# Block-sparse attention with a mixer MLP on one Trainium2 core: values of the later pairs by SyncE's queue and a GpSimd cast, and early value loads behind casts

## The chip, the cores and the metric

The kernel runs on 1 core of one Trainium2 chip. The metric is the time of one execution on the device, in microseconds (us). Engines are named as in the profile: PE (TensorE matmul), PEld (its weight loads), DVE (VectorE), ACT (ScalarE), POOL (GpSimd) and SP (SyncE, which only issues transfers here). Each engine works through its own list of instructions in order. Transfers are issued by SP and by POOL; both feed the same 16 DMA engines.

## The reference, cut to what matters

The first part is attention for 4 batches of 8 heads, 768 rows of 64; each query attends to the three best of its key blocks of 64 rows and to its own block, causally. The second is a token and channel mixer over its result.

```python
k_rep = k.reshape(B, H, n_blocks, block, D).mean(axis=3)
gate_scores = np.einsum('bhsd,bhnd->bhsn', q, k_rep)       # top 3 causal blocks + own block -> mask
scores = scale * np.matmul(q, k.transpose(0, 1, 3, 2))     # masked, causal
attn = np.exp(scores - max); attn = attn / sum
x = np.matmul(attn, v)                                     # -> (4, 768, 512)
h = np.maximum(x.transpose(0, 2, 1) @ w_tok1, 0.0) @ w_tok2
u = x + h.transpose(0, 2, 1)
out = u + np.maximum(u @ w_ch1, 0.0) @ w_ch2
```

q, k, v and the weights come as float32; the kernel computes in float16 with float32 sums.

## The kernel before

The work is cut into 16 pairs of heads, `pairs[i] = (b, h)`, numbered 0 to 15; four pairs make a batch. For each pair `prepare(i)` makes these operations:

- **Loads.** SP loads the keys `kl` and the queries `ql` as float32 (L313, two transfers of 192 KB each, one for each head; runs of 256 bytes). POOL loads the values `V` (L320, one transfer that casts to float16 on the way, straight into `V16[i % 6]`).
- **Transposes.** PE transposes `kl` and `ql` (L358, six blocks each) into a PSUM tile of the ring `big`, which has two places. ACT copies it to `kt` or `qt` (L367; rings of two and four). POOL casts `kt` and `qt` to float16 into `KA` and `QA` (L374, two casts each, one for each head).
- **Gate.** DVE sums blocks of keys (L387, L395), PE multiplies (L405, or L415 and L435 for groups of pairs), DVE finds the third best block (L447 to L483), PE turns the mask (L493) and DVE puts it into `QA` (L499).

`attend(i)` follows: scores on PE (L513), exponentials on ACT (L526), the diagonal mask on DVE (L533), `e` times `V` on PE (L545), and the division (L553, L564). The mixer of a finished batch (`tok1` L576 and L607, `umix` L588 and L621, `ch1` L657, `ch2` L678) is interleaved on PE with the attention of later pairs; its weights come by ten POOL transfers that also cast (L706, L707, L709, L711), one of 768x256, one of 256x768, four of `wc1` and four of `wc2`.

No loop sets the order. `plan()` works it out when the program is built: it takes the operations with their dependences, an occupation in ns, a due time (`prio`) and the rings that they take, and starts on each engine what is ready first, ties within 60 ns going to the smaller due time. A transfer has a `size`, which is the time that the planner gives it on the DMA engines; `transfers()` shares them between POOL's and SP's queue by `SHARE`. `casts` after `WAIT[n]` hold each weight transfer back; a line after the loops holds each value load behind a transpose of queries, `O["tr", "ql", d]`. SP's operations are started strictly in the order of due times. Where PE has nothing ready, the planner puts in multiplications of a tile of zeros (L695, tile `warm`); they stand in PE's list from then on. The resulting order is emitted under a manual schedule, so on the chip each engine follows it whatever the actual times are; the waits come from the tiles' uses. Each transfer by SP waits for the one eight places before it on SP's queue, since eight semaphores go round.

Two rings matter around the change: `V16` has six places, so the values of pair i can't be written before `e` times `V` of pair i-6 is done; `kt` has two, so the copy to `kt` of pair i waits for both casts of pair i-2.

Of the kernel before, what the change touches and what calls it, by code (L numbers as in the profile page):

```python
# [9 lines left out]
FP = mybir.dt.float32  # L10
# [18 lines left out]
R = 5  # L29
NBN = 4  # L30
# [9 lines left out]
def QACT(i):  # L40
    return i < 1


GATE = {2: 700, 3: 700, 4: 730}
GROUPED = [[0], [1], [2], [3], [4], [5], [6, 7], [8, 9, 10, 11], [12, 13, 14, 15]]
WAIT = [("kt", 3, 1), ("kt", 3, 1), ("qt", 3, 1), ("qt", 3, 1), ("qt", 4, 1), ("qt", 4, 1),
        ("qt", 5, 1), ("qt", 5, 1), ("qt", 6, 1), ("qt", 6, 1)]
# [171 lines left out]
def kernel(  # L219
# [11 lines left out]
    nc = tc.nc  # L231
    B, H, S, D = q.shape
    NB = S // 64
    NJ = S // 128
# [12 lines left out]

    pairs = [(b, h) for b in range(B) for h in range(0, H, 2)]
    NP = len(pairs)
    RINGS = dict(big=2, bank=3, av=1, ql=3, kl=3, qt=4, kt=2, gs=1, gt=1, gm=1, m8=1, bn=NBN, e0=3, e1=3, e2=3, rc=2,  # L250
                 x16=2, h1=2, u=2, uT=2, h2=1, ob=3)

    def sb(tag, shape, dt, name):
        return sp.tile(shape, dt, tag=tag, bufs=RINGS[tag], name=name)

    def ps(tag, shape, name, dt=FP):
        if tag == "big":
            return pp.tile([128, 1024], FP, tag=tag, bufs=RINGS[tag], name=name)
        return pp.tile(shape, dt, tag=tag, bufs=RINGS[tag], name=name)


    avp = pp.tile([128, 512], FP, tag="av", bufs=1, name="avp")
    V16 = [sp.tile([128, 2, NJ, 65], F16, tag=f"V{r}", name=f"V{r}") for r in range(R + 1)]
# [23 lines left out]
    T = {}  # L287
# [3 lines left out]
    def op(eng, occ, rec, deps, prio, fn, takes=(), size=0):  # L291
        o = Op(eng, occ, rec, deps, prio, fn, takes, size)
        ops.append(o)
        return o

    def pe(occ, deps, prio, fn, takes=(), tail=170):
        return op("PE", occ, occ + tail, deps, prio, fn, takes)

    def act(cols, deps, prio, fn, takes=()):
        return op("ACT", 70 + cols * 0.833, 173 + cols * 0.833, deps, prio, fn, takes)  # L300
# [5 lines left out]
    def load_qk(i, t32, src):  # L306
        b, h = pairs[i]

        def f():
            t = sb(t32, [128, NJ, 2 * D], FP, f"{t32}_{i}")  # L310
            T[t32, i] = t
            for g in range(2):
                nc.sync.dma_start(out=t[:, :, D * g:D * g + D], in_=src[b, h + g].rearrange("(j p) d -> p j d", p=128))  # L313
        return f

    def load_v(i):
        b, h = pairs[i]

        def f():
            nc.gpsimd.dma_start(out=V16[i % (R + 1)].rearrange("p g j d -> p (g j) d")[:, :, 0:D],  # L320
                                in_=v[b, h:h + 2].rearrange("g (j p) d -> p (g j) d", p=128))
        return f


    def load_gate_consts():
# [195 lines left out]
    def expo(i, x, g):  # L521
        def f():
            width = GROUPS[g][0]
            e = sp.tile([128, 1024 if g < 2 else 640], F16, tag=f"e{g}", bufs=RINGS[f"e{g}"], name=f"e{g}_{i}_{x}")
            T["e", i, x, g] = e
# [23 lines left out]
    def recip(i, x):  # L549
        def f():  # L550
            rc = sp.tile([128, NJ, 1], FP, tag="rc", bufs=RINGS["rc"], name="rc")
            T["rc", i, x] = rc
            nc.vector.reciprocal(out=rc.rearrange("p n o -> p (n o)"),  # L553
                                 in_=T["aps", i, x][:, :, 64:65].rearrange("p n o -> p (n o)"))
# [143 lines left out]
    O = {}  # L698
# [13 lines left out]
    W = []  # L712

    def prepare(i):
        b, h = pairs[i]
        gi = [n for n, G in enumerate(GROUPED) if i in G][0]
        i0 = GROUPED[gi][0]
        pre = 10.0 * (i0 - (AHEAD if i < FIRST else LATER)) + 2.5 * (i - i0) - (0 if len(GROUPED[gi]) == 1 else EXTRA)
        vpre = 10.0 * (i - (AHEAD if i < FIRST else LATER))
        old = i - R  # L720

        def last_scores(x):
            return [O.get(("sc", old, x, g)) for g in range(3)]

        for t32, src, off in (("kl", k, 0), ("ql", q, 0.1)):
            bf = Buf(t32)
            O[t32, i] = op("SP", 950, 0, [], pre - 12 + off, load_qk(i, t32, src), [bf], size=1750)
            big = Buf("big")
            O["tr", t32, i] = pe(660, [O[t32, i]], pre + off, transposes(t32, i), [big], tail=320)
            bf.users.append(O["tr", t32, i])  # L730
            name = "kt" if t32 == "kl" else "qt"
            tb = Buf(name)
            O[name, i] = act(768, [O["tr", t32, i]],
                             pre + 0.5 + off, evac_t(t32, i), [tb])
            big.users.append(O[name, i])
            dst = KA if name == "kt" else QA
            for x in range(2):
                occ = 770
                if QACT(i):
                    O["cast", name, i, x] = act(768, [O[name, i]] + last_scores(x), pre + 0.9 + 0.2 * x + off, cast_act(dst, name, i, x))  # L740
                    tb.users.append(O["cast", name, i, x])
                    continue
                O["cast", name, i, x] = op("POOL", occ, occ + 55, [O[name, i]] + last_scores(x), pre + 4 + off,
                                           cast(dst, name, i, x))
                tb.users.append(O["cast", name, i, x])
            if name == "kt":
                O["ksum", i] = dve(870, [O["kt", i]], pre + 1, ksum(i))
                tb.users.append(O["ksum", i])
                O["kcopy", i] = dve(200, [O["ksum", i], O.get(("gate", old))], pre + 1, kcopy(i))
            else:  # L750
                qb = tb
        O["v", i] = op("POOL", 1060, 0, [O.get(("av", i - R - 1, x)) for x in range(2)], vpre + 2, load_v(i), size=1350)
        n = len(GROUPED[gi])
        O["qb", i] = qb
        if i == GROUPED[gi][-1]:
            G = GROUPED[gi]
            if n == 1:
                gb = Buf("bank")
                O["gate", i] = gate_op = pe(1120, [O["kcopy", i], O["qt", i]], pre + 2, gate(i), [gb])
            else:  # L760
                tbig = Buf("big")
                gate_op = pe(GATE[n], [O["kcopy", m] for m in G] + [O["qt", m] for m in G], pre + 2, gate_t(gi), [tbig])
                for m in G:
                    O["gate", m] = gate_op
                gtb = Buf("gt")
                ge = act(S - 128, [gate_op], pre + 2.1, gate_e(gi), [gtb])
                tbig.users.append(ge)
                gb = Buf("big")
                gback = pe(550, [ge], pre + 2.2, gate_b(gi), [gb])
                gtb.users.append(gback)  # L770
            for m in G:
                O["qb", m].users.append(gate_op)
            gs = Buf("gs")
            O["gm", gi] = dve(75 + 125 * n, [gate_op] if n == 1 else [gback, own_op], pre + 3, gm(gi), [gs])
            gb.users.append(O["gm", gi])
            tops = [dve(720, [O["gm", gi]], pre + 3, top(gi, s)) if s == 0 else None for s in range(n)]
            for s in range(1, n):
                tops[s] = dve(720, [tops[0]], pre + 3, top(gi, s))
            O["lt", gi] = dve(75 + 125 * n, tops, pre + 3, below(gi))
            O["bias", gi] = dve((75 + 125 * n) if n == 4 else 200 * n, [O["lt", gi], O.get(("mask", gi - NBN))] + ([own_op] if n == 4 else []), pre + 3, bias(gi))  # L780
            gs.users += [O["bias", gi]]
            O["lt", gi].two = O["bias", gi].two = True
            mb = Buf("bank")
            O["mask", gi] = pe(280, [O["bias", gi]], pre + 4, mask(gi), [mb])
            for s, m in enumerate(G):
                for x in range(2):
                    O["put", m, x] = dve(410, [O["mask", gi]] + [O.get(("sc", m - R, x, g)) for g in range(3)],
                                         pre + 4, put_mask(gi, s, x))
                    mb.users.append(O["put", m, x])
# [38 lines left out]
        for i in G:  # L828
            attend(i)

    for i, d in enumerate((1, 2, 2, 3, 3, 4, 4, 5, 6, 7, 8, 9, 10, 11, 12, 13)):
        O["v", i].deps.append(O["tr", "ql", d])
    own_op.deps.append(O["cast", "qt", 4, 1])
    for x in range(2):
        O["cast", "kt", 0, x].deps.append(O["qt", 0])
    O["ksum", 1].deps.append(O["bias", 0])
    for n, (at, f) in enumerate(wq):
        W.append(op("POOL", 700, 0, [O[("cast",) + WAIT[n]]], at, f, size=4500 if n < 2 else 2100))

    for b in range(B):  # L840
        fill = 1000.0 * (b + 1)
# [5 lines left out]
        if b == 0:  # L847
            for c in range(4):
                bk = Buf("bank")
                at = fill + c  # L850
# [65 lines left out]
    kernel_plan.update(ops=O)  # L916
    order, span = plan(ops, RINGS)

# [65 lines left out]
```

The softmax here doesn't subtract the row's maximum and nothing guards it: scores larger than these inputs give would overflow.

## Time and profile before

| what | us |
|---|---|
| median of 12 runs | 265.87 |
| lowest and highest of them | 265.2 and 268.87 |
| the profiled execution's own time | 267.72 |
| its span in the trace | 265.6 |
| PE busy | 255.7 (96%) |
| DVE, ACT, POOL busy | 159.1, 145.2, 80.0 |
| SP's queue: packets, MB, share of 16 DMA engines | 63232, 21.33, 39.1% |
| POOL's queue: the same | 28064, 7.08, 27.0% |

The span is the trace's; the rest of an execution's own time lies before its first and after its last instruction. Lines of the profile name an instruction by its line of the kernel, engine, and tiles written and read. A DMA share is the sum of the packets' times over the 16 engines, divided by the time, so it exceeds 1 where packets of two queues overlap. MB and GB/s count the bytes as written, so a transfer of values to float16 counts half of what it reads.

### The profile page before, as it was taken

To read this page: it belongs to the slowest core of one execution; us is meant where nothing else is said; L and a number is where in the kernel's file an instruction comes from. 1 tells how busy PE (TensorE), PEld (TensorE's weight loads), DVE (VectorE), ACT (ScalarE), POOL (GpSimd) and SP (SyncE) were. 2 spreads that over 40 slices of the span, in tenths; PEclk is the share of its full clock that TensorE was granted. 3 is DMA by queue.
4 is the path that set the end of the run, shared out by engine and by line. 5 is a ranking of instruction groups with operands and counts; after the bars stand their busy time and mean duration, and the time that the engine had idled before them with its cause. 6 is when DMAs were issued, how large, how long until landed. Compare 5 with 4: busy or idle time off the path is not lost.

```text
span 265.6 us, 5842 instructions
## 1 busy us (share of the span) xinstructions
PE 255.7 (96%) x2304; PEld 166.2 (63%) x2304; DVE 159.1 (60%) x536; ACT 145.2 (55%) x195; POOL 80.0 (30%) x112
## 2 busy tenths in 40 slices
PE   7889999999996999999999999999999999999994
PEld 7777888895765767455666676655456544456443
DVE  4668869896974769986547975493233153333222
ACT  3757898677894966457873599860024400044000
POOL 8494819849445745225520000000000000000000
PEclk9999999999999999999999999999999999999999
DMA  8999999999997999059511000009220026310032
GB/s 170 204 169 189 177 180 208 192 188 193 192 151 141 211 205 174 21 78 171 69 45 41 1 2 0 2 0 187 92 79 2 0 46 152 119 41 0 2 141 96
DMA packets 91322, 28.77 MB, mean 108 GB/s; under 512 B 84896, under 2 KB 87840, under 8 KB 91296
## 3 DMA queue, kind: packets, MB, share of 16 engines
q1 hardware_dynamic: 63232, 21.33, 39.1%
q0 software_dynamic: 28064, 7.08, 27.0%
q8 instruction: 18, 0.29, 0.5%
q14 instruction: 8, 0.07, 0.1%
HBM read 26.83 MB, written 6.29 MB: 125 GB/s over the span
## 4 chain that ended last, share of the span: by engine, by line
PE 86%; DMA 8%; SPq 3%; DVE 2%; issue 1%; DVEq 0%
PE c L678 23%; PE c L657 23%; PE sps L513 13%; DMA kl<-in_k_dram 8%; PE avp L545 7%; PE ups L588 3%; PE tkl L358 3%; PE tql L358 3%; PE tok L576 2%; SPq L313 2%; PE gps L405 2%; PE gtp L415 1%; PE tok L607 1%; PE bps L493 1%; PE avp L695 1%; PE ups L621 1%
## 5 line engine op out<-in xcount | busy, mean ns | idle before, releaser
L526 ACT ACTIVATE e<-sps 128x1024 f16<-128x1024 f32 (+1 forms) x96 | 84.3, 920 | 17.3 <-PE sps L513 14.0
L657 PE MATMUL c<-uT,wc 128*128 128x256 f16 (+1 forms) x384 | 69.1, 326 | 0.0
L678 PE MATMUL c<-wc,h 128*128 128x512 f16 (+2 forms) x300 | 65.6, 370 | 0.0
L667 ACT ACTIVATE h<-c 128x512 f16<-128x512 f32 x48 | 28.7, 598 | 61.1 <-PE c L657 42.9
L657 PEld LDWEIGHTS <-wc 128*128 128x128 f16 x384 | 36.5, 97 | 23.0 <-issue 0.2
L513 PE MATMUL sps<-QA,KA 88*128 88x512 f16 (+3 forms) x256 | 50.1, 305 | 0.0
L678 PEld LDWEIGHTS <-h 128*128 128x128 f16 x300 | 28.7, 98 | 30.5 <-issue 1.0
L533 DVE TENSOR_TENSOR e<-e,m 128x256 f16<-128x256 f16 x90 | 30.0, 341 | 14.3 <-ACT e L526 13.8
L374 POOL CAST KA<-kt 64x768 f16<-64x768 f32 x30 | 24.7, 824 | 45.8 <-ACT kt L367 28.8
L686 DVE TENSOR_TENSOR ob<-u,c 128x512 f32<-128x512 f16 (+2 forms) x25 | 16.5, 664 | 32.1 <-PE c L678 32.1
L669 DVE TENSOR_SCALAR h<-c 128x256 f16<-128x256 f32 x48 | 20.3, 422 | 25.7 <-PE c L657 25.3
L513 PEld LDWEIGHTS <-KA 88*128 88x128 f16 x256 | 23.1, 99 | 17.0 <-issue 0.7
L374 POOL CAST QA<-qt 64x768 f16<-64x768 f32 x30 | 25.6, 852 | 6.1 <-ACT qt L367 4.7
L545 PEld LDWEIGHTS <-e 128*128 128x128 f16 x672 | 25.4, 97 | 2.8
L545 PE MATMUL avp<-V,e 128*128 128x65 f16 x672 | 26.7, 193 | 0.0
L367 ACT COPY kt<-tkl 128x768 f32<-128x768 f32 x16 | 12.8, 799 | 14.8 <-PE tkl L358 7.2
L387 DVE TENSOR_REDUCE kst<-kt 128x12 f32<-128x768 f32 x16 | 15.2, 950 | 8.2 <-ACT kt L367 8.0
L564 DVE TENSOR_TENSOR x<-avp,rc 128x384 f16<-128x384 f32 x32 | 17.8, 555 | 0.8
L320 POOL DMA_DIRECT2D V<-in_v_dram x16 | 16.5, 1035 | 5.6 <-PE avp L545 3.4
L358 PE MATMUL tkl<-id,kl 128*128 128x128 f32 x96 | 13.6, 277 | 4.2 <-DMA kl<-in_k_dram 4.2
L499 DVE COPY QA<-bps 24x640 f16<-24x640 f16 x32 | 14.3, 480 | 2.2 <-PE bps L493 1.9
L367 ACT COPY qt<-tql 128x768 f32<-128x768 f32 x16 | 12.8, 802 | 3.7 <-PE tql L358 3.5
(66 smaller groups left out, 212.3 us busy)
## 6 DMA issues: line engine op xcount, KB each, us to landing
kl<-in_k_dram SPq DMA_DIRECT2D x32, 192.0 KB, 5.7
ql<-in_q_dram SPq DMA_DIRECT2D x32, 192.0 KB, 5.8
out_dram<-ob SPq DMA_DIRECT2D x23, 256.0 KB, 2.0
V<-in_v_dram POOLq DMA_DIRECT2D x16, 192.0 KB, 8.5
wc<-in_moe_w_ch_dram POOLq DMA_DIRECT2D x8, 384.0 KB, 12.4
w<-in_moe_w_tok_dram POOLq DMA_DIRECT2D x2, 384.0 KB, 9.8
out_dram<-ob SPq DMA_DIRECT2D x1, 160.0 KB, 1.8
out_dram<-ob SPq DMA_DIRECT2D x1, 96.0 KB, 1.7
```

Of the source, the lines that this page charges most:

```text
L358: nc.tensor.transpose(out=p[:, 128 * j:128 * j + 128], in_=t[:, j, :], identity=ident32)
L367: nc.scalar.copy(out=t, in_=p[:, 0:S])
L374: nc.gpsimd.tensor_copy(out=to, in_=src)
L513: nc.tensor.matmul(out=p[:, off + a:off + a + n], lhsT=KA[i % R][x][0:MK, 128 * kk:128 * kk + 128], rhs=QA[i % R][x][0:MK, q0 + a:q0 + a + ...
L526: nc.scalar.activation(out=e[:, 0:width], in_=T["sps", i, x, g][:, 0:width], func=AF.Exp, scale=scale)
L533: nc.vector.tensor_tensor(out=d, in0=d, in1=m0.rearrange("p (a b) -> p a b", a=1).broadcast_to([128, 2, 128]), op=ALU.mult)
L545: nc.tensor.matmul(out=p[:, jq, :], lhsT=T["e", i, x, g][:, o:o + 128], rhs=V16[i % (R + 1)][:, x, kk, :], start=(kk == 0), stop=(kk == jq))
L564: nc.vector.tensor_tensor(out=T["x16", b][:, :, 64 * hh:64 * hh + 64], in0=T["aps", i, x][:, :, 0:64], in1=T["rc", i, x].broadcast_to([128 ...
L657: nc.tensor.matmul(out=p, lhsT=wc1_16[:, cc, 128 * fc:128 * fc + 128], rhs=T["uT", b][:, cc, a // 128:e // 128, :], start=(cc == 0), stop= ...
L667: nc.scalar.activation(out=T["h2", b][:, fc, a:e], in_=T["c1", b, fc, n], func=AF.Relu)
L669: nc.vector.tensor_scalar(out=T["h2", b][:, fc, a:e], in0=T["c1", b, fc, n], scalar1=0.0, scalar2=None, op0=ALU.max)
L678: nc.tensor.matmul(out=T["c2", b, j, lo], lhsT=T["h2", b][:, fc, 128 * j:128 * j + 128], rhs=wc2_16[:, fc, lo:hi], start=(fc == 0), stop=( ...
```

## The change

Three things change. The values of pairs 8 to 15 are loaded as float32 by SP into a new ring `v32` with two places (in SP's order right after the queries of the same pair), and POOL casts them into `V16`. The values of pairs 0 to 7 still come by POOL with the cast on the way, but each now waits for a given cast on POOL (`VAFTER`) instead of a transpose of queries. The `size` with which the planner counts the later weight transfers goes from 2100 to 2400 (`wc1`) and 2800 (`wc2`).

```diff
+VHW = 8
+VAFTER = [("kt", 1), ("kt", 2), ("qt", 2), ("qt", 3), ("qt", 3), ("kt", 4), ("qt", 4), ("qt", 5)]
...
-    RINGS = dict(big=2, bank=3, av=1, ql=3, kl=3, qt=4, kt=2, gs=1, gt=1, gm=1, m8=1, bn=NBN, e0=3, e1=3, e2=3, rc=2,
+    RINGS = dict(big=2, bank=3, av=1, ql=3, kl=3, qt=4, kt=2, v32=2, gs=1, gt=1, gm=1, m8=1, bn=NBN, e0=3, e1=3, e2=3, rc=2,
...
         def f():
-            nc.gpsimd.dma_start(out=V16[i % (R + 1)].rearrange("p g j d -> p (g j) d")[:, :, 0:D],
-                                in_=v[b, h:h + 2].rearrange("g (j p) d -> p (g j) d", p=128))
-        return f
+            src = v[b, h:h + 2].rearrange("g (j p) d -> p (g j) d", p=128)
+            if i < VHW:
+                nc.gpsimd.dma_start(out=V16[i % (R + 1)].rearrange("p g j d -> p (g j) d")[:, :, 0:D], in_=src)
+                return
+            T["v32", i] = sb("v32", [128, 2 * NJ, D], FP, f"v32_{i}")
+            nc.sync.dma_start(out=T["v32", i], in_=src)
+        return f
+
+    def cast_v(i):
+        return lambda: nc.gpsimd.tensor_copy(out=V16[i % (R + 1)].rearrange("p g j d -> p (g j) d")[:, :, 0:D], in_=T["v32", i])
...
-        O["v", i] = op("POOL", 1060, 0, [O.get(("av", i - R - 1, x)) for x in range(2)], vpre + 2, load_v(i), size=1350)
+        last_av = [O.get(("av", i - R - 1, x)) for x in range(2)]
+        if i < VHW:
+            O["v", i] = op("POOL", 1060, 0, last_av, vpre + 2, load_v(i), size=1350)
+        else:
+            vb = Buf("v32")
+            O["vl", i] = op("SP", 700, 0, [], pre - 11.8, load_v(i), [vb], size=1750)
+            O["v", i] = op("POOL", 820, 870, [O["vl", i]] + last_av, vpre + 2, cast_v(i))
+            vb.users.append(O["v", i])
...
-    for i, d in enumerate((1, 2, 2, 3, 3, 4, 4, 5, 6, 7, 8, 9, 10, 11, 12, 13)):
-        O["v", i].deps.append(O["tr", "ql", d])
+    for i, (name, m) in enumerate(VAFTER[:VHW]):
+        O["v", i].deps.append(O["cast", name, m, 1])
...
-        W.append(op("POOL", 700, 0, [O[("cast",) + WAIT[n]]], at, f, size=4500 if n < 2 else 2100))
+        W.append(op("POOL", 700, 0, [O[("cast",) + WAIT[n]]], at, f, size=4500 if n < 2 else 2400 if n < 6 else 2800))
```

## Prediction

> **What bounds the kernel now.** I read the busy times first, then the chain of waits, then PE's idle time, then the DMA engines in stretches of 4 us. PE is 96% busy, so what can be won is its idle time and its filler.
>
> ```profile
> PE 255.7 (96%) x2304; PEld 166.2 (63%) x2304; DVE 159.1 (60%) x536; ACT 145.2 (55%) x195; POOL 80.0 (30%) x112
> ...
> PE tkl L358 <- DMA kl<-in_k_dram: 4.2, 3, 2.3
> ```
>
> PE waits for a load of keys three times, 4.2 us together. The chain shows the places: before the transposes of pairs 2, 10 and 15.
>
> ```profile
> 7.54 6.09 DMA kl<-in_k_dram
> 13.77 0.85 PE tkl L358 x6
> ...
> 75.09 8.69 DMA kl<-in_k_dram
> 83.92 0.84 PE tkl L358 x6
> ...
> 99.52 6.13 DMA kl<-in_k_dram
> 105.79 0.84 PE tkl L358 x6
> ...
> 135.15 0.66 PE tql L358 x6
> ```
>
> The waits are 1.37, 2.34 and 0.46 us. The last line is the transposes of pair 15's queries, 29 us after its keys: PE asks for those late. From 107 to 144 PE shows 36.97 busy of 37 us, and from 144 to 181 36.97 of 37. So what PE loses up to 107 it doesn't get back, and what it gains it keeps.
>
> The DMA engines, by stretches (the last column is GB/s):
>
> ```profile
> 4.00:8.00 4.00, 3.81 (x52) 3.50 (x51) 1.27 (x3) 1.52 (x3) 4.00 (x5) 1.00 1.30 231
> 72.00:76.00 4.00, 4.00 (x43) 2.60 (x42) 3.70 (x10) 3.06 (x5) 3.82 (x5) 1.00 1.19 139
> 76.00:80.00 4.00, 4.00 (x47) 2.86 (x46) 2.39 (x8) 3.93 (x6) 0.25 (x1) 1.00 1.43 170
> 80.00:84.00 4.00, 1.66 (x31) 1.56 (x30) 2.24 (x7) 1.50 (x2) 2.60 (x4) 1.00 0.69 126
> 84.00:88.00 4.00, 4.00 (x29) 2.74 (x30) 2.31 (x5) 3.16 (x5) 2.46 (x4) 1.00 0.94 194
> 88.00:92.00 4.00, 4.00 (x37) 3.01 (x36) 2.72 (x6) 3.76 (x6) 2.60 (x4) 1.00 0.93 190
> 92.00:96.00 4.00, 4.00 (x50) 2.16 (x47) 2.33 (x6) 3.15 (x5) 3.19 (x4) 1.00 1.23 227
> 96.00:100.00 4.00, 4.00 (x49) 3.39 (x47) 2.92 (x25) 2.31 (x5) 1.01 (x1) 1.00 1.60 192
> 100.00:104.00 4.00, 4.00 (x32) 3.28 (x31) 4.00 (x26) 2.16 (x3) 3.61 (x4) 1.00 1.55 198
> ```
>
> SP alone moves 227 to 231 GB/s when it doesn't stop (4 to 8, 92 to 96). Beside values by POOL, whose float16 bytes count half, a full stretch shows 192 to 198. The DMA engines are thus full nearly all of the time up to 105, and short of it only from 72 to 92. Both bounds meet at 100 to 107: PE and the loads finish the attention's inputs together.
>
> **What a value load costs on each queue.** By SP, 393 KB (two times 192 KB) at 229 GB/s are 1.72 us of all engines. By POOL: from 96 to 104 the engines wrote 1560 KB; the loads of pairs 12 and 13 (issued 94.3 and 98.7, landed 5.9 and 6.6 later) lie nearly whole in it with 393 KB; the other 1167 KB at 229 are 5.1 us, which leaves 2.9 us for two, 1.45 each. Moving one from POOL to SP thus *adds* 0.27 us of DMA work. The Trainium skill weighs in here, "DMA: Bandwidth & Descriptors", section "Issuing engines are not separate DMA queues": transfers of all issuing engines interleave on the same 16 engines, so moving one saves issue time only. By that rule the price would be 0 a load instead of 0.27, and the sum below 1.6 us lower.
>
> **First part, early values held back.** Before, values 0 go out at 7.01 and share the engines with keys 2. After, in the order of the built program, POOL issues them after three casts: 11.87 + 3 x 0.85 = 14.4. Keys 2 (second half issued at about 7.4) come without them: values 0 had 5.5 us from issue to the last byte, and 1.45 us of that was theirs, so keys 2 land up to 1.4 sooner; PE's filler ends at 12.33, so 1.2 of the 1.37 is won. Values 0 then land at 14.4 + 6.0 (the row of values 1, issued at 15.29) = 20.4. PE wants them at 21.75 before; after, 1.2 sooner, but behind 7 + 1 instead of 2 multiplications of zeros (6 x 0.054) and keys 3's transposes (0.69), at 21.5. The cover is 1 us; between the fastest and slowest lone row (4.2 and 6.4) they land at 18.6 to 20.8. Values 1 and 2 are wanted after 29 and land at 25 to 28. PE's list has 128 multiplications of zeros for 136: 8 x 0.054 = 0.43 us less. First part: PE is 1.6 us ahead at 60 (0.5 to 2.4: values 0 late by 1; or also the 0.8 us of waits for DVE at 20.13 and 50.77 gone). All of it is only a lead; whether it lasts is decided below.
>
> **Second part, POOL's casts.** No value cast is in the trace. Nearest are the casts of 64x768 float32, 0.82 and 0.85 us. I take 0.85, since a partition has as many elements; bounds 0.82, and 1.7 if twice the partitions took twice as long. Each takes the place of an issue of 1.02 us: 8 x (0.85 - 1.02) = -1.4 us of POOL, bounds -1.6 and +5.4, and POOL is 30% busy. Not the length counts but the wait ahead: a cast of values stands in POOL's list until its load has landed. The list runs values 8, 9, keys and queries 8, values 10, 11, keys and queries 9 and 10, values 12, and so on. Keys 9 free a place of `kt`, and ACT's copy of keys 11 waits for it, with the exponentials queued behind. SP's list is queries 11, then values 11. Before, queries 11 land at about 89.3 (issued until 85.8, 4.1 to landing). After, values 8 to 11 add 4 x 0.27 = 1.1, and DMA idle time got back (below) takes 1.8: values 11 land at 88.6, their cast and the two of keys 9 end at 91.2, ACT copies keys 11 at 91.2 instead of 90.01. Before, PE goes on with scores at 91.28; after, it needs that copy done, 92.0, with 0.66 us of `e` times `V` done ahead. So here the lead of 1.6, and the 2.34 won at keys 10 (which go ahead of values 10 and 11), is spent: at 92 PE is level, +0.1 us (bounds -2 to +1.7, with the landing 2 sooner or the casts 1.7 long).
>
> **Third part, the end of the loads.** In PE's list the transposes of queries 15 now come right after those of keys 15, not 29 us later. In the old program that place is 105.79 + 0.68 = 106.4, and the end of those transposes would be 107.1. Before, queries 15 landed at about 106.6 (issued 100.23 to 101.5, 6.2 and 5.2 to landing), and nothing waited. What is different in DMA work ahead of them:
> - values 14, which before are issued at 120, are now ahead in SP's list: +1.72 us;
> - values 8 to 13 by SP: 6 x 0.27 = +1.6;
> - idle time of 72 to 92 that may be got back: 4 x (1 - 126/227) = 1.8 at 80 to 84, 1.2 and 0.6 at 72 to 80 against 198, 0.6 and 0.6 at 84 to 92: 4.8 us in all.
>
> How much of the 4.8 returns is the unknown. From 72 to 84 (3.6 us) values by POOL flew beside SP, which the change removes, but SP's own issues also stood up to 5 us there; from 84 to 92 SP was alone and still 15% short, so that share stays. I take half of the first: 1.8; bounds 0 and 4.8. Queries 15 land at 106.6 + 1.7 + 1.6 - 1.8 = 108.1 (105.1 to 109.9), their transposes end 0.1 + 0.66 later at 108.9, against 107.1: **+1.8 us** (level or ahead at the lower bound, +3.6 at the upper). PE's order behind it is dense as before, so this stays to the end. The weights' new sizes only shift places in the list: the ten transfers and their bytes are the same, and `wc2`, wanted at 101, landed at 74 before; 27 us cover it. Cost 0.
>
> **Sum.** In the profile's terms 265.6 + 1.8 = 267.4 of span. That execution took 267.72 (2.1 around the span), 1.85 above the median of 265.87; the difference goes on the median: 265.87 + 1.8 = **267.7**.
>
> **Rivals.**
> - *Idle time returns in full, faster.* With POOL's values gone SP runs at 227 throughout. Then values 11 land 2 us sooner, queries 15 at 105.1, and PE keeps a lead: filler 0.43, keys 2 1.2, keys 10 2.34, keys 15 0.46, together 4.4, less 1 to 2 at keys 11. 265.9 - 3 = 262.9. For: 92 to 96 at 227. Against: 84 to 92. Chance 0.28.
> - *Gains and waits cancel.* Three fifths to four fifths of the 4.8 return: queries 15 land within 0.7 us of where PE wants them, 265.2 to 267. So does a change that only exchanges one queue for the other, by the rule above. Chance 0.22.
> - *POOL's list is the stop, slower.* If casts of values take 1.7 us or values 9 and 11 land 2 us later than reckoned, keys 8 and 9 are cast later, ACT stands at the copies of keys 10 and 11 and PE with it: 2 x 0.85 + 2 = 3.7 more in that stretch, of which the lead has already been spent: 269.6. It decides once values 11 land after 90. Chance 0.12.
> - The forecast, queries 15 late by 0.5 to 3: chance 0.38.
>
> About 0.5% (1.3 us) is what a measurement of this kernel tells from no change. Faster by more 0.28, within 0.22, slower 0.50 (the forecast and POOL's stop). Range 262.8, just below the rival's 262.9, to 270.6 (3.6 of late queries and 1.1 of POOL).
>
> **What would show it.** The trace after should show keys 2's wait under 0.4 us; no wait of PE for keys 10; ACT's copy of keys 11 after a cast on POOL; a wait of PE before transposes of queries at 105 to 109; GB/s from 72 to 104 near 200. I am wrong if PE doesn't wait there (SP's queue was faster than I price it), or if `e` times `V` of pair 0 waits for values 0, or if GB/s stays at 225 from 70 on.

## The result and the profile after

| | before | after |
|---|---|---|
| median | 266.48 (47 runs, 265.15 to 268.87) | 270.01 (11 runs, 268.07 to 271.82) |
| ratio | | 1.0127, interval 1.0098 to 1.0156 |
| the profiled execution: own time, span | 267.72, 265.6 | 270.01, 268.0 |

The change makes the kernel 1.3% slower: +3.5 us, where +1.8 was forecast.

First the busy times, the queues and PE's waits of the changed kernel (line, what it waited for, us in all, times, longest):

```profile
PE 255.5 (95%) x2296; PEld 165.9 (62%) x2296; DVE 160.3 (60%) x536; ACT 145.1 (54%) x195; POOL 78.8 (29%) x112
...
q1 hardware_dynamic: 75648, 24.48, 45.9%
q0 software_dynamic: 15648, 5.51, 17.5%
...
PE tql L367 <- DMA ql<-in_q_dram: 3.5, 3, 1.7
PE sps L522 <- ACT kt L376: 2.2, 1, 2.2
...
PE tkl L367 <- DMA kl<-in_k_dram: 0.6, 1, 0.6
```

PE's own work is the same as before, 255.5 us against 255.7. What changed is what it stands still for: keys cost 4.2 us before and 0.6 now, but queries cost 3.5 and scores that stand behind ACT's copy of keys another 2.2, both new. The timeline of PE says where (start, duration, and in brackets the idle time ahead and what ended it; transposes of keys are `tkl`, of queries `tql`):

```profile
67.87 0.82 PE L367 MATMUL tkl<-id,kl 128*128 128x128 f32 x6
70.43 0.85 PE L367 MATMUL tql<-id,ql 128*128 128x128 f32 x6 [1.75 <-DMA ql<-in_q_dram]
...
81.29 0.82 PE L367 MATMUL tkl<-id,kl 128*128 128x128 f32 x6
...
92.02 0.59 PE L522 MATMUL sps<-QA,KA 88*128 88x512 f16 x3 [2.23 <-ACT kt L376]
98.29 0.85 PE L367 MATMUL tkl<-id,kl 128*128 128x128 f32 x6
...
103.92 0.85 PE L367 MATMUL tql<-id,ql 128*128 128x128 f32 x6 [0.74 <-DMA ql<-in_q_dram]
106.96 0.85 PE L367 MATMUL tkl<-id,kl 128*128 128x128 f32 x6 [0.62 <-DMA kl<-in_k_dram]
108.78 0.85 PE L367 MATMUL tql<-id,ql 128*128 128x128 f32 x6 [0.97 <-DMA ql<-in_q_dram]
```

These are pair 8 (the first two lines), keys 10, the scores at the copy of keys 11, keys 12, queries 14, and keys and queries 15. Keys 8 start at 67.87, 2.0 us ahead of the 69.90 of before; the lead is gone at queries 8, one line down. At keys 12 PE is where it was before, 98.29 against 98.23. The two lines of before:

```profile
69.90 0.87 PE L358 MATMUL tkl<-id,kl 128*128 128x128 f32 x6
...
98.23 0.85 PE L358 MATMUL tkl<-id,kl 128*128 128x128 f32 x6
```

The last three stops, 2.33 us together, put the end of pair 15's transposes at 108.78 + 0.69 = 109.5, and nothing behind it makes that good: 109.5 - 107.1 = 2.4 is the whole difference of the two spans.

The chain of waits shows what stands behind the two large stops (start, duration, what):

```profile
57.22 13.08 DMA ql<-in_q_dram
...
82.57 5.96 DMA v<-in_v_dram
...
88.66 0.83 POOL V L331
89.49 0.77 POOL KA L383
...
90.31 0.84 POOL KA L383
...
91.17 0.81 ACT kt L376
...
92.02 0.59 PE sps L522 x3
...
104.47 4.18 DMA ql<-in_q_dram
...
108.78 0.85 PE tql L367 x6
```

From 82.57 to 92.02 one can read the new dependence as a single line of work: values 11 land, POOL casts them, only then casts the two heads of keys 9, ACT copies keys 11 into the place that this frees, PE goes on. PE won't need values 11 until much later; they only stand ahead of something that it needs. The last two lines are the end of the loads: queries 15 are issued at 104.47 and PE takes them 0.13 us after they land.

The DMA engines in stretches of 4 us (PE busy is the second number, GB/s the last):

```profile
68.00:72.00 4.00, 2.25 (x22) 1.75 (x21) 1.34 (x5) 2.08 (x3) 0.20 (x1) 1.00 0.61 137
72.00:76.00 4.00, 4.00 (x44) 2.58 (x42) 3.86 (x10) 2.76 (x5) 0.63 (x1) 1.00 1.00 212
76.00:80.00 4.00, 4.00 (x49) 3.02 (x47) 3.16 (x11) 3.90 (x6) 2.62 (x4) 1.00 1.14 230
...
88.00:92.00 4.00, 1.79 (x32) 1.68 (x31) 0.27 (x1) 1.27 (x3) 3.22 (x4) 1.00 1.15 231
...
100.00:104.00 4.00, 3.26 (x26) 2.48 (x24) 4.00 (x27) 2.23 (x4) 3.76 (x6) 1.00 1.00 181
104.00:108.00 4.00, 3.18 (x23) 2.08 (x23) 3.91 (x9) 2.10 (x3) 1.85 (x2) 1.00 1.13 231
```

In 88 to 92 and 104 to 108 the DMA engines run at 231 GB/s, the most that any stretch of 4 us of this execution shows, while PE has 1.79 and 3.18 of 4 us to do. In 104 to 108 the transfers are what is late; in 88 to 92 they are until values 11 land at 88.53, and from there to 92.02 it is the casts and the copy behind them. In 68 to 72 both stand partly still.

### The profile page after: what moved, and what is told of

It is laid out like the page before. It is cut to its first block, busy times and chain, and to the rows that moved or that the text cites. A ratio compares the mean times of both kernels' runs of the same rounds, so it can differ in the third digit from the quotient of the medians.

```text
span 268.0 us, 5836 instructions
## 1 busy us (share of the span) xinstructions
PE 255.5 (95%) x2296; PEld 165.9 (62%) x2296; DVE 160.3 (60%) x536; ACT 145.1 (54%) x195; POOL 78.8 (29%) x112
## 4 chain that ended last, share of the span: by engine, by line
PE 85%; DMA 9%; SPq 1%; ACT 1%; POOL 1%; issue 1%; DVEq 0%; DVE 0%; POOLq 0%; ACTq 0%
PE c L687 23%; PE c L666 20%; PE sps L522 12%; PE avp L554 7%; DMA ql<-in_q_dram 6%; PE avp L704 3%; PE tql L367 3%; PE ups L597 3%; PE tkl L367 3%; PE gps L414 2%; PE tok L585 2%; DMA v<-in_v_dram 2%; SPq L315 1%; PE bps L502 1%; PE tok L616 1%; PE ups L630 1%
## 5 line engine op out<-in xcount | busy, mean ns | idle before, releaser
L522 PE MATMUL sps<-QA,KA 88*128 88x512 f16 (+3 forms) x256 | 49.4, 306 | 2.8 <-ACT kt L376 2.2
L542 DVE TENSOR_TENSOR e<-e,m 128x256 f16<-128x256 f16 x90 | 30.9, 349 | 15.2 <-ACT e L535 14.4
L383 POOL CAST KA<-kt 64x768 f16<-64x768 f32 x30 | 25.3, 843 | 32.4 <-PE sps L522 16.4
L367 PE MATMUL tql<-id,ql 128*128 128x128 f32 x96 | 13.5, 276 | 4.3 <-DMA ql<-in_q_dram 3.5
```

What stands on the lines that cost most here:

```text
L367: nc.tensor.transpose(out=p[:, 128 * j:128 * j + 128], in_=t[:, j, :], identity=ident32)
L383: nc.gpsimd.tensor_copy(out=to, in_=src)
L522: nc.tensor.matmul(out=p[:, off + a:off + a + n], lhsT=KA[i % R][x][0:MK, 128 * kk:128 * kk + 128], rhs=QA[i % R][x][0:MK, q0 + a:q0 + a + ...
L542: nc.vector.tensor_tensor(out=d, in0=d, in1=m0.rearrange("p (a b) -> p a b", a=1).broadcast_to([128, 2, 128]), op=ALU.mult)
```

## The experiments

Twelve kernels. Times are medians of ten runs, of eleven for the changed kernel (`after`), and of four for the three rows with the weights' sizes, the cast of values 11 and the load of values 14; a ratio is against the kernel before, with its 95% interval.

| kernel | us | ratio, interval |
|---|---|---|
| after | 270.01 | 1.0127, 1.0098 to 1.0156 |
| first part alone | 266.86 | 1.0017, 0.9987 to 1.0046 |
| second part alone | 269.42 | 1.0118, 1.0076 to 1.0159 |
| after, weights' sizes as before | 270.78 | 1.0137, 1.0083 to 1.0191 |
| after, queries 15 late | 268.82 | 1.0094, 1.0067 to 1.0121 |
| after, cast of values 11 later | 269.45 | 1.0107, 1.0061 to 1.0154 |
| after, load of values 14 later | 269.96 | 1.0126, 1.0075 to 1.0178 |
| after, both of these | 268.06 | 1.0051, 1.0015 to 1.0087 |
| after, all SP value loads three pairs later | 265.22 | 0.9951, 0.992 to 0.9982 |
| before, late values held back only | 266.34 | 1.0002, 0.9959 to 1.0045 |
| the same with the first part | 264.84 | 0.9932, 0.9888 to 0.9976 |
| the same, held back longer | 264.63 | 0.9915, 0.9878 to 0.9953 |

The theory at the start: the loss is the *place* of the later values in two lists that run in order, SP's (ahead of keys and queries that PE wants sooner) and POOL's (ahead of the casts of keys). The rivals: SP's queue is dearer in itself; holding the early values back costs; the weights' new sizes cost.

**First part alone**, in the kernel before (the later values as before):

```diff
-    for i, d in enumerate((1, 2, 2, 3, 3, 4, 4, 5, 6, 7, 8, 9, 10, 11, 12, 13)):
-        O["v", i].deps.append(O["tr", "ql", d])
+    for i, (name, m) in enumerate(VAFTER):
+        O["v", i].deps.append(O["cast", name, m, 1])
+    for i, d in enumerate((6, 7, 8, 9, 10, 11, 12, 13)):
+        O["v", i + 8].deps.append(O["tr", "ql", d])
```

> The kernel before with the early value loads (pairs 0 to 7) held behind casts as in the change; values 8 to 15 by POOL as before, weights' sizes as before. Theory of the loads' end: the first part wins a lead (keys 2 no longer waited for, some 1.2 us; PE some 1.6 us ahead at 60) that the wait for keys 10 takes back, since the DMA engines carry the same bytes until then: keys 10 land at 83 to 84 as before, time within 1 us of the kernel before (265.5 to 267.0). Rival, the early loads are the loss: e times V of pair 0 or 4 waits for values, and it is as slow as the changed kernel, 269 or more.

266.86, no difference that can be told. In its profiled execution, the slowest of the ten, PE is ahead at keys 8 (68.78 against 69.90) and then waits 2.58 us for keys 10, at 83.03. So the first part isn't the loss, and its lead is spent where the loads are late.

**Second part alone**: the changed kernel with the early values tied to transposes and the weights' sizes as in the kernel before.

```diff
-    for i, (name, m) in enumerate(VAFTER[:VHW]):
-        O["v", i].deps.append(O["cast", name, m, 1])
+    for i, d in enumerate((1, 2, 2, 3, 3, 4, 4, 5)):
+        O["v", i].deps.append(O["tr", "ql", d])
```

> The changed kernel with the early value loads and the weights' sizes as before, so that only values 8 to 15 by SP with the cast are new (the planner puts queries 15 late on PE here). Theory of the two stops: POOL's list still has values 11 ahead of keys 9, so PE waits some 2 us for ACT's copy of keys 11 (without the early loads' lead PE comes later, so 1 to 2.2), and keys 15 land with values 14 ahead: 267.5 to 269.5. Rival, the early loads behind casts made the loss: 266.3, as before.

269.42: moving the later values to SP brings a loss without the rest of the change. Its profiled execution is one of its shorter ones (span 266.8, the median of its ten is 267.7), and there the planner has put pair 15's transposes at 129.5, so queries 15 are no stop; values 11 land by 86.43, 2.2 us sooner than in the changed kernel, and PE doesn't stop for the copy of keys 11, where a wait was expected. What that execution lost is something else: PE was busy 258.6 us, 2.9 more than before, since its clock was at half from 19.6 to 26.5, ahead of any load of the later values (see the last section). Nine of the ten runs had a lowered clock, but it isn't the whole loss: the one at full clock took 269.22. What the longer executions lose, that trace can't tell. So this run shows which part loses, not by which stop.

**The weights' sizes** as before, all else as changed (`size=4500 if n < 2 else 2100`):

> The changed kernel with the weights' sizes as in the kernel before (2100 for all eight later transfers). SP's and POOL's lists are the same as the changed kernel's, only PE's, DVE's and ACT's orders around the mixer of batch 0 differ a little. Theory: both stops stay, 269 to 270.5. Rival, the sizes cost something through PE's order: below 268.5.

270.78, just above what was expected, and the interval covers that of the changed kernel: the sizes are not the loss. The trace repeats the stop at the copy of keys 11. Here no queries 8 were late and PE came to it with its lead, yet it went on at nearly the same moment:

```profile
91.57 1.01 PE L522 MATMUL sps<-QA,KA 88*128 88x512 f16 x3 [3.99 <-ACT kt L376]
```

91.57 against 92.02, with 3.99 us of idle time ahead in place of 2.23. A stop of this kind is a point in time set by POOL's list and the landing ahead of it; coming sooner only makes the wait longer.

**The two stops taken away, one at a time and together.** Queries 15 kept until late in PE's list, as in the kernel before:

```diff
+    O["tr", "ql", 15].deps.append(O["sc", 11, 0, 0])
```

> The changed kernel, with the transposes of queries 15 held behind scores of pair 11, so that PE asks for them some 28 us after those of keys 15, as in the kernel before; nothing else is edited. Theory of the loads' end: the wait of 0.97 us for queries 15 goes, the one of 0.6 for keys 15 stays: span 267.0, 1.0 below the changed kernel's 268.0; time near 269.0. Rival, the wait behind values 11 on POOL is what costs: no change, 268.0 and 270.0.

268.82. Queries 15 are transposed at 136.54 without a wait, and the stop for the copy of keys 11 is still there, 2.76 us. By the medians that gives back 1.2 of the 3.5 us (the intervals overlap a little).

The cast of values 11 put behind those of queries 10, so that it no longer stands ahead of keys 9:

```diff
+    O["v", 11].deps.append(O["cast", "qt", 10, 1])
```

> The changed kernel, with the cast of values 11 moved in POOL's list behind the casts of pairs 9 and 10; PE's order is the same. Theory of the loads' end: PE's wait of 2.2 us at 92 goes, but the lead of it is spent at the loads that follow (queries 14, keys 15, queries 15), whose landings don't move: those waits grow by as much, span 267.7 to 268.0, time 269.7 to 270. Rival, POOL's list is the stop: span 265.8, time near 267.8.

269.45, 0.6 us less by the medians, which the intervals can't tell from nothing. The stop at 92 is gone, keys 12 start at 95.66 instead of 98.29, and the 2.6 us are handed on to the end of the loads:

```profile
101.09 0.85 PE L367 MATMUL tkl<-id,kl 128*128 128x128 f32 x6 [1.20 <-DMA kl<-in_k_dram]
102.78 0.85 PE L367 MATMUL tql<-id,ql 128*128 128x128 f32 x6 [0.84 <-DMA ql<-in_q_dram]
106.37 0.85 PE L367 MATMUL tkl<-id,kl 128*128 128x128 f32 x6 [1.17 <-DMA kl<-in_k_dram]
108.19 0.85 PE L367 MATMUL tql<-id,ql 128*128 128x128 f32 x6 [0.97 <-DMA ql<-in_q_dram]
```

Four waits, 4.2 us, and queries 15 at 108.19 against 108.78. The load of values 14 put behind those of pair 15 instead:

```diff
-            O["vl", i] = op("SP", 700, 0, [], pre - 11.8, load_v(i), [vb], size=1750)
+            O["vl", i] = op("SP", 700, 0, [], pre - 11.8 if i != 14 else 100.65, load_v(i), [vb], size=1750)
```

> The changed kernel, with only the load of values 14 moved behind that of queries 15 in SP's list; PE's order is the same. Theory of the loads' end: keys 15 and queries 15 land 1.72 us sooner, the waits of 0.62 and 0.97 us for them go, span 266.4, 1.6 below 268.0; time near 268.4. Rival, not the bytes but SP's issues or the release of buffers by PE set those landings: they land as in the changed kernel, span 268.0.

269.96: nothing, and the expectation was missed. Keys and queries 15 are no longer waited for, but PE comes to them late, though it goes on from the stop at 92.02 exactly as the changed kernel does. Its PE between the two, in stretches of 2 us (the third number from the end is the granted clock):

```profile
90.00:92.00 2.00, 0.00 (x0) 0.00 (x0) 0.00 (x0) 0.83 (x2) 1.88 (x3) 1.00 1.18 229
92.00:94.00 2.00, 1.98 (x12) 1.18 (x12) 1.92 (x6) 2.00 (x3) 1.82 (x4) 0.87 1.20 215
94.00:96.00 2.00, 2.00 (x11) 0.49 (x13) 1.01 (x3) 1.19 (x2) 1.88 (x3) 0.50 1.18 210
96.00:98.00 2.00, 2.00 (x23) 0.92 (x16) 0.00 (x0) 0.72 (x2) 1.94 (x3) 0.77 1.29 235
```

After 2.08 us without work PE's clock is granted at half for some 3.4 us. Keys 12 start at 99.93 instead of 98.29: the 1.6 us that the later load won were lost here. All four of its runs had a lowered clock, so what this edit alone gives at full clock is not measured. Both edits together:

> The changed kernel with both edits that were made singly: the cast of values 11 behind the casts of pairs 9 and 10 on POOL, and the load of values 14 behind that of queries 15 on SP; PE's order is the same. Theory of two stops in a row: each edit alone moved the time by 0.6 us or less because the other stop takes over (POOL's list at 92, the end of the loads at 104 to 109). With both gone keys 15 and queries 15 land 1.7 sooner than in the kernel without the cast's stop (106.4 and 108.2) and PE is there: span 265.7 for 267.4, time near 267.7. Rival, the loss lies elsewhere (queries 8's wait at 70, the lowered clock): 269.5 as before.

268.06, 1.95 us less than the changed kernel, where one alone gave 0.6 and the other 0.05. The stops stand one behind the other and each hides what the other costs. (The profiled execution is the fastest of the ten, 266.35.) This pair also measures what a value load on SP costs: from keys 14 to queries 15, both waited for, the kernel with values 14 between them takes 108.19 - 101.09 = 7.10 us, and without them:

```profile
99.78 0.85 PE L367 MATMUL tkl<-id,kl 128*128 128x128 f32 x6 [1.89 <-DMA kl<-in_k_dram]
...
105.12 0.85 PE L367 MATMUL tql<-id,ql 128*128 128x128 f32 x6 [0.52 <-DMA ql<-in_q_dram]
```

5.34 us; the difference is 1.76 us for 393 KB.

**Place or queue.** All values of pairs 8 to 15 still by SP and cast by POOL, but three pairs later in SP's list (those of pairs 13 to 15 behind queries 15):

```diff
-            O["vl", i] = op("SP", 700, 0, [], pre - 11.8, load_v(i), [vb], size=1750)
+            j = min(i + 3, 15)
+            at = 10.0 * ({8: 8, 9: 8, 10: 8, 11: 8}.get(j, 12) - LATER) + 2.5 * (j - (8 if j < 12 else 12)) - EXTRA
+            O["vl", i] = op("SP", 700, 0, [], at - 11.85 + 0.01 * (i - 8), load_v(i), [vb], size=1750)
```

> The changed kernel with each value load by SP put three pairs later in SP's list (values 8 behind queries 11, and so on, values 13 to 15 behind queries 15), casts on POOL placed by the planner accordingly. Theory of the changed kernel's two stops: casts no longer wait for loads on POOL, and three value loads fewer stand ahead of queries 15 (5.2 us): PE waits neither at 92 nor at the end of the loads; span 262.5 to 264.5, time 264.5 to 266.5, better than the kernel before or level with it. Rival, values by SP are dear wherever they stand: 268 or more.

265.22: 4.8 us less than the changed kernel, and 0.5% below the kernel before, with the same transfers by the same queue and the same casts. PE waits for no load; before queries 15 it waits 0.98 us, for ACT:

```profile
102.98 0.88 PE L367 MATMUL tql<-id,ql 128*128 128x128 f32 x6 [0.98 <-ACT kt L376]
```

The loss was the place (the planner orders PE's work a little differently with it, too). The queue and the cast are not dear in themselves.

Then the other half: all values by POOL as in the kernel before, but the later ones held until transposes of keys 11 to 15, first without and then with the first part of the change:

```diff
-    for i, d in enumerate((1, 2, 2, 3, 3, 4, 4, 5, 6, 7, 8, 9, 10, 11, 12, 13)):
+    for i, d in enumerate((1, 2, 2, 3, 3, 4, 4, 5)):
         O["v", i].deps.append(O["tr", "ql", d])
+    for i, d in enumerate((11, 12, 13, 14, 15, 15, 15, 15)):
+        O["v", i + 8].deps.append(O["tr", "kl", d])
```

> The kernel before with values 8 to 15 by POOL held back until the transposes of keys 11 to 15 (as in the run with 264.84), early value loads as before. Theory: the early loads' lead of 1.2 to 1.6 us, worth nothing while the end of the loads set the time, is missing here where it doesn't: 266.0 to 266.5, 1.2 to 1.6 above 264.84. Rival: the loads' end was all, and the early part is worth nothing in any setting: 264.8.

> The kernel before with early values behind casts as in the change, and values 8 to 15 still by POOL with the cast on the way but held back until the transposes of keys 11, 12, 13, 14 and 15 (values 12 to 15 also keys 15). Theory, the DMA engines carry values too early: with four value loads (5.8 us of DMA work) out of the way keys 10 aren't waited for, PE idles nowhere for 2 us from 60 to 100, its lead of some 1.6 us and the 2.3 of keys 10 hold to the end: span 261.5 to 263, time 263.5 to 265, below the kernel before (266.3). Rival, SP's queue by itself sets the landings, whatever POOL does: no better than 266. It is wrong too if e times V of pair 8 waits for its values (wanted at 116, issued near 89).

266.34 and 264.84. Holding back the later values alone gives nothing that can be told; the first part on top of it lowers the median by 1.5 us (the intervals overlap a little), where alone it gave nothing. In the first of the two PE comes to keys 10 at 82.10 and to keys 15 at 102.97, in the second at 79.54 and 100.41, and in neither does it wait for a load there. So the lead of the first part is kept once no load stops PE later. Held back longer, with the first part (values 8 from keys 13, 9 from keys 14, all others from keys 15):

```diff
-    for i, (t, d) in enumerate([('kl', 11), ('kl', 12), ('kl', 13), ('kl', 14), ('kl', 15), ('kl', 15), ('kl', 15), ('kl', 15)]):
+    for i, (t, d) in enumerate([('kl', 13), ('kl', 14), ('kl', 15), ('kl', 15), ('kl', 15), ('kl', 15), ('kl', 15), ('kl', 15)]):
```

> The same as the last, but values 8 held until the transposes of keys 13, values 9 of keys 14 and values 10 to 15 of keys 15. Keys and queries have the DMA engines for themselves until 100. Theory, the DMA engines carry values too early: the same or up to 1 us better than the last, 262.5 to 265; queries 15, which PE's order has early again here, land by 102 and aren't waited for. Rival: values 8 to 10 then come late, e times V of pair 8 waits at 115, slower than the last by 1 to 3.

264.63, the best version, 0.85% below the kernel before, though its interval and those of the kernel with the shorter hold and of the one with SP's values three pairs later overlap. Three of its stretches, to be held against those of the changed kernel above:

```profile
88.00:92.00 4.00, 4.00 (x49) 2.16 (x46) 2.31 (x6) 3.15 (x5) 2.26 (x3) 1.00 0.77 160
92.00:96.00 4.00, 4.00 (x50) 3.38 (x48) 2.95 (x25) 2.31 (x5) 0.02 (x1) 1.00 0.02 4
96.00:100.00 4.00, 4.00 (x33) 3.25 (x32) 4.00 (x26) 2.33 (x4) 3.90 (x5) 1.00 1.03 204
```

PE is busy throughout, and for 4 us the DMA engines move next to nothing (4 GB/s): with the values out of the way the loads have time to spare in the very place where the changed kernel is short of it.

**The kernel before once more**, unchanged, to see which of its waits are steady:

> The kernel before once more, unedited, for a second trace: the first profiled execution (span 265.6) was longer than most of its runs (263.0 to 265.7). Theory: keys 10 and keys 15 landed sooner in the shorter ones; in this trace PE waits less than the 2.34 and 0.46 us there, and a span near 264 has about 1.5 us less of PE's waits for keys. Rival: the waits are the same and the difference lies in the granted clock or elsewhere.

Span 264.6. Keys 10 are transposed at 81.64 without a wait and keys 15 at 104.36 without one, where the profiled execution that the prediction read had waited 2.34 and 0.46 us; a wait of 1.12 us for ACT stands ahead of queries 10 instead:

```profile
81.64 0.84 PE L358 MATMUL tkl<-id,kl 128*128 128x128 f32 x6
84.91 0.84 PE L358 MATMUL tql<-id,ql 128*128 128x128 f32 x6 [1.12 <-ACT h L667]
...
104.36 0.84 PE L358 MATMUL tkl<-id,kl 128*128 128x128 f32 x6
```

PE's waits for keys are 1.1 us in all instead of 4.2, but the span is only 1.0 us shorter, since other waits stand in their place. So two of the waits that the change was to win (keys 10 and 15) are not there in every execution.

## Why the prediction was right in its sign and half its size

**Right, step by step.**
- Keys 2 are no longer waited for, values 0 came in time (`e` times `V` of pair 0 starts at 20.64 without a wait), and PE was 2.0 us ahead at keys 8 (1.6 forecast at 60).
- A cast of values takes 0.83 us, between the two rows that the prediction went by (0.82 and 0.85).
- Values 11, their cast, keys 9, the copy of keys 11: forecast 88.6, 91.2 and PE at 92.0; measured 88.53, 91.15 and 92.02. PE level afterwards: forecast +0.1, measured 98.29 - 98.23 = +0.06.
- The waits at the end of the loads came where they were put, before pair 15's transposes. Those of queries 15 ended at 109.5 (108.9 forecast). The 0.6 us lie within the bounds given for the idle time that returns: queries 15 landed at 108.65, so by the forecast's own terms 106.6 + 1.7 + 1.6 - 108.65 = 1.3 us came back where 1.8 were taken. From 72 to 104 the engines moved 211 GB/s on average (near 200 forecast).
- A value load by SP costs 1.76 us (1.72 forecast). The other half of the 0.27, the load by POOL at 1.45, no run measured by itself, so the 0.27 stays an estimate.
- That PE's order is dense behind pair 15 held: the delay of 2.4 us there is the difference of the spans.

**The step that failed is the sum.** The forecast put +1.8 on the median ("the difference goes on the median"), since the profiled execution was 1.85 us above it. But the new stop is a landing, which comes at nearly its own time whether PE is early or late: with the cast of values 11 later PE came to keys 12 2.6 us sooner, but to queries 15 only 0.6 us sooner (108.19 against 108.78). The 1.85 us of that long execution were in good part waits ahead of it (keys 10 and 15), and the change was forecast to replace these. Put on the execution that it was worked out from, the sum is 267.72 + 1.8 = 269.5, and 270.01 was measured. The second look at the kernel before shows the same from the other side: there pair 15's keys start at 104.36, so the place for queries 15 would end at 104.36 + 0.68 + 0.66 = 105.7, and 109.5 - 105.7 = 3.8 us, where the medians of all runs differ by 3.5. So of the 1.7 us that were missing, about 1.4 are the base (107.1 - 105.7) and 0.6 the landing; that is 0.3 too much, since single executions stand here beside medians.

**Missed without harm.** The wait for queries 8 (1.75 us) was not foreseen: after the issue of values 8 SP stood 7.76 us at keys 9 while queries 8 took 13.08 us from issue to landing. It took the lead 22 us before the place where the forecast had it spent; without it (the kernel with the old sizes) the stop at the copy of keys 11 takes it. The lowered clock was not foreseen either, and is told below.

**The rivals.** Idle time did not return in full: 211 GB/s from 72 to 104, not 227, and no lead was left. POOL's list was a stop, as the forecast had it, and values 11 landed before 90. If moving a load between the queues cost nothing, the forecast's sum would have left PE nearly level. It wasn't level, but that doesn't decide the price, of which only SP's half was measured. The kernel with later places shows why it hardly mattered: what costs 1.76 us costs it only ahead of something that PE wants.

**Still open:** how the 3.5 us split among the stops. Queries 15 late gave 1.2, values 11 and 14 together 1.95, and all values later 4.8, which holds the first part's lead too; these don't add, since each stop hides part of the next. The wait for queries 8 was taken away by no edit of its own.

## What to carry to other kernels

Where the DMA engines are full, the order of the transfers is what counts: put first what the bounding engine wants first, and leave what is wanted late until the loads have time to spare, on whichever queue. An operation that waits for a transfer makes everything behind it on its engine wait too, so place it by when its data land, behind the work that others wait for. A delay that ends in a landing is reckoned from the time of the landing, not as an addition to the median; and a wait that one execution shows is not yet one to win, so look at a second.

## What the runs showed that was not expected

After some of its stops PE's granted clock fell to half. It stayed there for 3.4 us or twice that (read from stretches of 0.5 us): 84.3 to 87.75 after the wait of 2.58 us in the first part alone, 92.8 to 96.2 after 2.76 us with queries 15 late, 93.5 to 96.9 after 2.08 us with values 14 late, and 90.5 to 97.3 with the old sizes, where it began within the wait of 3.99 us. But the changed kernel's profiled execution had none after 2.23 us, nor had the kernel before's after 2.34 us. And in the second part alone it came with two waits of only 1.06 us (at 13) and 0.99 us (at 20):

```profile
18.00:20.00 2.00, 1.41 (x14) 1.12 (x13) 1.86 (x10) 1.55 (x2) 1.88 (x3) 0.91 1.89 180
20.00:22.00 2.00, 1.59 (x10) 1.00 (x11) 1.83 (x13) 0.16 (x1) 1.04 (x2) 0.50 1.87 172
22.00:24.00 2.00, 2.00 (x21) 1.56 (x20) 0.79 (x3) 1.42 (x2) 0.00 (x0) 0.50 1.35 228
24.00:26.00 2.00, 2.00 (x21) 1.94 (x19) 0.83 (x3) 0.64 (x1) 0.00 (x0) 0.50 0.95 194
```

The second look at the kernel before has waits of 1.05 and 0.98 us in the same two places and no lowered clock. So the length of a stop alone doesn't decide.

Where PE has work without a gap a stretch of 3.4 us at half clock costs 1.7 us by this arithmetic; 1.64 was measured (keys 12, above). The runs' mean clocks show how often: traces with one such stretch have means of 0.992 or 0.993, those with two 0.985 or 0.986 (1 - 1.7 / 268 is 0.994). Of the changed kernel's 11 runs 9 were below 0.998, five of them at 0.987. Of the 69 runs of the kernel before beside the experiments 34 were, and of the 30 runs of the three kernels that beat it, 2. Yet the clock is not what makes the changed kernel slower: its two runs at full clock took 270.01 and 270.56 us, where the kernel before's 35 at 0.998 or more have a median of 265.89.

The Trainium skill, "TensorE: Matmul & The Clock Gate", section "Part 1: The HAM clock gate (the "warmup" mystery)", gives free-running windows of about 3.4 us and half rate after at least one idle window. The length agrees with the stretches here; but shorter stops were enough, 2.08 us in one execution and about 1 us in another, while 2.23 and 2.34 us had no such effect in others. By these runs a wait of PE of a microsecond or more can be dearer than its length, by up to 1.7 us for each stretch at half clock; whether one follows could not be foretold here.
